# A planner with another model of TensorE's clock, new due dates, and dummy matmuls that share the banks of the attention steps

## The chip, the cores and the metric

The kernel runs on one core of one Trainium2 chip. The time is the device time of one execution in microseconds; the kernel before takes 923.4 us (median of three runs, 922.99 to 923.58).

## What is computed

Attention over q, k, v of shape (4, 8, 576, 64), followed by two MLPs over the 2304 tokens of width 512. The attention is a sum of two parts: one over positions averaged four by four (144 of them, repeated four times at the end), and one in a band of seven positions around each token.

```python
q_d, k_d, v_d = (x.reshape(B, H, S // 4, 4, D).mean(axis=3) for x in (q, k, v))
out_up = np.repeat(sm_attn(q_d, k_d, v_d), 4, axis=2)
mask = np.abs(pos[:, None] - pos[None, :]) < 4
scores = np.where(mask, scale * q @ k.T, -1e9)
out_local = softmax(scores) @ v
x = (out_up + out_local).transpose(0, 2, 1, 3).reshape(2304, 512)
r = np.maximum(x @ w_in, 0.0)               # 512 -> 2048
x = (s * (r * r) + b) @ w_out               # 2048 -> 512
out = ((x @ w_a) * (x @ w_b)) @ w_out2      # 512 -> 1536 -> 512
```

## The kernel before

**The stages.** The *ramp* computes, on TensorE, the averaged attention of batch 0 and batch 1 (`down`, one group for each of four pairs of heads) and the banded attention of the first 768 tokens in six *tile jobs* of 128 tokens (`tile_job`). Tile jobs 0 to 2 fill block 0 of phase A, jobs 3 to 5 block 1. Jobs 0 to 3 lie in batch 0 and read q and k of that batch from buffers that `down` loaded; jobs 4 and 5 load their own (`tq`, `tk`). The band of the other tokens is computed on VectorE (`unit`), beside phase A; each unit visits TensorE for a transpose (`bt`). *Phase A* is the first MLP: six blocks of 384 tokens, each with 16 steps of the hidden width, each step 12 matmuls into `h` (`h_fn`, lines 1154 to 1156) and, two steps later, 12 into `acc` (`o_fn`, lines 1197 to 1199). *Phase B* is the second MLP (line 1443 and lines 1583 to 1585). A value is split into a high and a low fp32r part, and a product is three matmuls: high by high, high by low, low by high.

**The weights.** For block 0 of phase A each of the 32 weight slices (512 KB) comes by SyncE's queue and is split on ScalarE (lines 416, 423 and 452) and VectorE (lines 428, 436 and 457). At most four slices are staged between their transfer and line 436 (the token `stg`). Slices, whole q and k of batch 0 and some other tiles of the ramp share the 33 slots of the pool `w`.

**Steps on TensorE in the ramp.** A down group has scores (`sc`, line 690), transposes (`at`, line 741) and the output (`o`, line 762, evicted at 774 into `up`). A tile job has scores (lines 854 and 862), transposes (line 928) and the output (line 947); VectorE adds `up` (line 964), and the sum is split into `xsh` (ScalarE, line 571) and `xsl` (VectorE, line 575). That is the x that phase A reads.

**The order.** All work stands in a list of tasks (`Program.add`), each with an engine, a planned duration, what it reads, which buffers it takes and gives back, and a due time. `Program.order` plays the list through before the kernel is emitted: it takes again and again the task that can start earliest on its engine, on a tie the one with the smaller due time (less `LEAD` for TensorE's attention steps), and emits in that order. Each engine's queue, SyncE's too, is then run in order by the chip, with semaphores where one engine needs another. Due times are handed back from a task to those that it needs. `target(idx)` is the due time of step idx of phase A: `T0` plus `STEP` per token and step; the jobs' due times hang on it by the constants `DUE_*`.

**PSUM and the dummies.** The eight banks are two `att`, two `h` and four `acc`. An attention step of the ramp takes any of them. `warm_fn` takes one acc bank as `pw` and emits 18 dummy matmuls (bf16, 408 columns) into it; the bank comes free with the first product of phase A. Up to that product `order` also puts dummies ahead of any TensorE step which, by the plan, would otherwise start late: as many as end before the step can start, 20 at most. `Clock` is the plan's model of TensorE's clock: a step runs at full or half speed by what the tick before it did.

Of the kernel before, what the change touches and what calls it, by code (L numbers as in the profile page):

```python
# [7 lines left out]
F32 = mybir.dt.float32  # L8
# [9 lines left out]
HP = H // 2  # L18
# [42 lines left out]
V_ENG = "DDDD"  # L61
POOL_PREP = 2.0
CONST_ENG, DUE_CONST = "G", 8.0
PATIENCE = 0
# [26 lines left out]
class Task:  # L91
    __slots__ = (
        "eng", "dur", "fn", "deps", "succ", "acq", "picks", "rel", "due", "lead", "share", "num", "left", "ready", "start",
        "end", "fill", "seen", "dma", "order", "wait",
# [3 lines left out]
class Clock:  # L98


    TICK, COLUMNS = 3.41333, 1.4

    def __init__(self):
        self.done = {}

    def run(self, start, work, share, keep=True):
        t = start
        while work > 1e-9:
            k = int(t / self.TICK + 1e-6)
            rate = 1.0 if self.done.get(k - 1, 0.0) >= self.COLUMNS else 0.5  # L110
            d = min(work / rate, (k + 1) * self.TICK - t)
            if keep:
                self.done[k] = self.done.get(k, 0.0) + d * rate * share
            work -= d * rate
            t += d
        return t


# [18 lines left out]
class Program:  # L137
# [7 lines left out]

    def add(self, eng, dur, fn, reads=(), writes=(), acq=(), rel=(), due=1e9, after=(), lead=0.0, share=1.0, seen=None, dma=(), order=0, wait=0.0):
# [5 lines left out]
        t.lead, t.share = lead, share  # L152
# [12 lines left out]

    def order(self):
# [8 lines left out]
        at = {e: 0.0 for e in ENGINES}  # L175
        clock, warming, wire = Clock(), True, Wire()
        landed, adding = [], 0.0
        at["SP"] = 0.75
        at["PE"] = clock.run(1.07, 0.17 * WARM, 1.0)
        out = []  # L180
# [107 lines left out]
def moe_chain(ctx, tc, qT, kT, vd, tq, tk, tv, qu, ku, vu, w_a1, w_o1, w_a2, w_b2, w_o2, sb, ident_d, bmask_d, emask_d, out):  # L288
    nc = tc.nc
# [5 lines left out]
    add = P.add  # L295
# [33 lines left out]

# [14 lines left out]
    def warm_fn(picks):  # L344
        V.memset(wz, 0.0)
        pw.append(bank("acc", [128, 408], "pw"))
        keep_warm(WARM)
        V.memset(ones, 1.0)
        A_.activation(out=warm, in_=ones, func=ACTF.Exp)
# [17 lines left out]

    add("CTL", 0.0, warm_fn, acq=[("acc",)], due=-1e6)

# [262 lines left out]
    def down(b, hp, ph, pool_eng, due=1e9):  # L632
# [53 lines left out]
        def s_fn(p):  # L686
# [58 lines left out]

        tt = add("PE", 0.52, t_fn, [("a", key), "ident"], [("at", key)], [wide, wide], lead=LEAD, share=0.5625)

# [9 lines left out]
        def o_fn(p):  # L757
# [9 lines left out]
        to = add(  # L767
            "PE", 2.1 if b == 0 and V_ENG[hp] == "P" else 0.6, o_fn, [("aT", key), ("upslot", b)] + [("dv", key) if b == 0 else ("pv", b)],
            [("o", key)], [wide], [pick(ts, 2)] + ([pick(tv0, 0)] if b == 0 else ["pv"] if hp == HP - 1 else []),
            lead=LEAD, share=0.5625, after=[mm["dO", b, i] for i in range(hp)])  # L770
        mm["dO", b, hp] = to
# [28 lines left out]
    def pick(t, i):  # L800
        return lambda _: t.picks[i]


    def tile_job(i, due):
# [44 lines left out]
        def s_fn(p):  # L849
# [21 lines left out]
            [("tsc", i)], [WIDE, WIDE, ("re",)], () if kept else ["rtq", "rtk"],  # L871
            after=[mm["dS", bl, hp] for hp in range(HP)], lead=LEAD, share=0.55,
        )
# [51 lines left out]
        def t_fn(p):  # L925
# [5 lines left out]
            "PE", 0.55, t_fn, [("ta", i)], [("tat", i)], [WIDE], after=[mm["dT", bl, hp] for hp in range(HP)],  # L931
            lead=LEAD, share=0.75,
        )
# [7 lines left out]
        def o_fn(p):  # L941
# [12 lines left out]
            "PE", 1.45, o_fn, [("taT", i), ("tv", i), ("slot", ("a", blk))] + [("up", b) for b in batches], [("to", i)], [WIDE, WIDE],  # L954
            [pick(ts, 2), pick(t_v, 0)], lead=LEAD, share=0.8,
        )
# [19 lines left out]
    def window(t, R):  # L976
        a = t.rearrange("p r d -> p (r d)")
        return bass.AP(tensor=a.tensor, offset=a.offset, ap=[list(a.ap[0]), [D, R], [D, 7], [1, D]])

    def unit(u, due):  # L980
# [110 lines left out]
        def bt(p):  # L1091
# [4 lines left out]
        tb = add(  # L1096
            "PE", 0.11 * R, bt, [("bo", u), ("slot", ("a", blk))] + [("up", b) for b in batches], [("bt", u)], [ONE],
            ["bo"], lead=LEAD,
        )
# [39 lines left out]
    def a_iter(idx):  # L1139
# [7 lines left out]
        for half in range(2):  # L1147
# [639 lines left out]
```

## Time and profile of the kernel before

| | us |
|---|---|
| median of three runs | 923.4 |
| the profiled execution | 923.98 |
| its span, first to last instruction | 922.2 |
| TensorE (PE) busy | 909.3, 99% |
| VectorE (DVE) busy | 777.4, 84% |
| ScalarE (ACT) busy | 476.2, 52% |
| GpSimd (POOL) busy | 71.8, 8% |
| mean granted TensorE clock | 0.982 of full speed |

In the page, PE is matmul, PEld the weight load beside it, and SPq SyncE's queue, which issues transfers. PEclk is the granted clock as a share of 2.4 GHz; it has two levels, 1.2 and 2.4 GHz, so a stage's value says how much of it ran at which. A matmul that stands in TensorE's queue without a gap counts as busy at either level, so that 99% busy doesn't mean 99% of what the engine could do. The busy time of an engine can hide dummies as well. The table is an average over stages; they are read one by one.

### The profile page before, as it was taken

What the parts mean: (1) busy time and instruction counts of PE and PEld (TensorE: products, weight loads), DVE (VectorE), ACT (ScalarE), POOL (GpSimd) and SP (SyncE); (2) the same over time, 40 slices, a digit from 0 to 9 for tenths busy, and PEclk for the clock granted to TensorE, in tenths of its full rate; (3) what the DMA queues carried; (4) which work ended last, traced back from release to release, by engine and by line L of the source; (5) the groups of instructions that cost most, each with busy time, mean ns of one, the idle gap of its engine ahead of it and who ended that gap; (6) DMA issues with size and microseconds to landing.
All of it is one profiled execution on the core that took longest, in us unless ns stands there. A gap on an engine that the chain in (4) does not pass through costs nothing.

```text
span 922.2 us, 15173 instructions
## 1 busy us (share of the span) xinstructions
PE 909.3 (99%) x5794; PEld 848.4 (92%) x5794; DVE 777.4 (84%) x1390; ACT 476.2 (52%) x1011; POOL 71.8 (8%) x74
## 2 busy tenths in 40 slices
PE   9989999999999999999999999999999999999997
PEld 5779999999999999999998999998999999999996
DVE  8699989999999999996877998779877779877753
ACT  4489974445445445337887454436433335433322
POOL 2310112034222100000000000000000000000000
PEclk9589999999999999999999999999999999999999
DMA  8986744233453323206487132102200000200001
GB/s 250 262 257 204 224 143 137 70 112 119 121 106 118 100 83 106 81 1 231 147 292 265 34 106 69 46 23 84 100 23 24 23 23 12 103 25 23 1 1 69
DMA packets 49224, 97.22 MB, mean 105 GB/s; under 512 B 6592, under 2 KB 24800, under 8 KB 48768
## 3 DMA queue, kind: packets, MB, share of 16 engines
q1 hardware_dynamic: 41520, 93.20, 30.8%
q0 software_dynamic: 7200, 2.67, 2.5%
q8 instruction: 45, 0.74, 0.3%
q10 hardware_dynamic: 432, 0.39, 0.1%
q14 instruction: 27, 0.22, 0.1%
HBM read 83.65 MB, written 12.58 MB: 104 GB/s over the span
## 4 chain that ended last, share of the span: by engine, by line
PE 90%; DVE 6%; ACT 2%; issue 1%; DVEq 0%; ACTq 0%
PE ab L1443 29%; PE h L1154 7%; PE acc L1197 7%; PE h L1155 6%; PE h L1156 6%; PE acc L1198 6%; PE acc L1199 6%; PE acc L1584 5%; PE acc L1585 5%; PE acc L1583 5%; PE pw L328 1%; PE o L762 1%; PE sc L690 1%; PE o L947 1%; PE at L741 1%
## 5 line engine op out<-in xcount | busy, mean ns | idle before, releaser
L1443 PE MATMUL ab<-xo,w 128*128 128x384 f32 x1312 | 267.7, 338 | 1.8 <-DVE w L1507 1.8
L1443 PEld LDWEIGHTS ab<-xo,w 128*128 128x128 f32 x1312 | 235.2, 188 | 16.9 <-DVE w L1507 2.1
L1197 PE MATMUL acc<-gh,w 128*128 128x384 f32 (+1 forms) x384 | 132.1, 344 | 1.5 <-DVE gh L1184 0.9
L1154 PE MATMUL h<-xsh,w 128*128 128x384 f32 x384 | 132.0, 344 | 0.1
L1198 PE MATMUL acc<-gl,w 128*128 128x384 f32 x384 | 129.9, 338 | 0.1
L1155 PE MATMUL h<-xsl,w 128*128 128x384 f32 x384 | 129.9, 338 | 0.0
L1156 PE MATMUL h<-xsh,w 128*128 128x384 f32 x384 | 129.6, 338 | 0.0
L1199 PE MATMUL acc<-gh,w 128*128 128x384 f32 (+1 forms) x384 | 129.5, 337 | 0.0
L1171 ACT ACTIVATE u<-h 128x384 f32<-128x384 f32 x96 | 47.2, 492 | 117.0 <-PE h L1156 113.4
L1559 ACT ACTIVATE gh<-u 128x384 fp32r<-128x384 f32 x68 | 35.7, 524 | 87.3 <-DVE u L1520 50.4
L1197 PEld LDWEIGHTS acc<-gh,w 128*128 128x128 f32 x384 | 72.1, 188 | 3.9 <-ACT w L423 2.0
L1154 PEld LDWEIGHTS h<-xsh,w 128*128 128x128 f32 x384 | 72.8, 190 | 2.2 <-issue 1.8
L1155 PEld LDWEIGHTS h<-xsl,w 128*128 128x128 f32 x384 | 72.9, 190 | 0.0
L1198 PEld LDWEIGHTS acc<-gl,w 128*128 128x128 f32 x384 | 72.2, 188 | 0.7 <-DVE gl L1182 0.7
L1156 PEld LDWEIGHTS h<-xsh,w 128*128 128x128 f32 x384 | 72.8, 190 | 0.0
L1199 PEld LDWEIGHTS acc<-gh,w 128*128 128x128 f32 x384 | 72.2, 188 | 0.0
L1467 ACT ACTIVATE w<-ab 128x384 f32<-128x384 f32 x34 | 16.7, 491 | 100.6 <-PE ab L1443 100.5
L1182 DVE TENSOR_TENSOR gl<-u,gh 128x384 fp32r<-128x384 f32 x96 | 53.6, 558 | 13.7 <-ACT gh L1178 13.3
L1175 ACT ACTIVATE u<-u 128x384 f32<-128x384 f32 x96 | 50.5, 526 | 2.0
L1178 ACT ACTIVATE gh<-u 128x384 fp32r<-128x384 f32 x96 | 50.5, 526 | 1.8
L1443 PE MATMUL ab<-xo,wx 128*128 128x384 f32 x200 | 50.0, 345 | 0.0
L1064 DVE TENSOR_TENSOR pr<-s,bk 128x1792 f32<-128x1792 f32 (+1 forms) x26 | 49.2, 1893 | 0.7
(208 smaller groups left out, 1724.9 us busy)
## 6 DMA issues: line engine op xcount, KB each, us to landing
w<-in_w_o_dram SPq DMA_DIRECT2D x25, 512.0 KB
w<-in_w_a_dram SPq DMA_DIRECT2D x24, 512.0 KB
bk<-in_ku_dram SPq DMA_DIRECT2D x22, 320.0 KB
bk<-in_vu_dram SPq DMA_DIRECT2D x22, 320.0 KB
w<-wod SPq DMA_DIRECT2D x12, 512.0 KB
x2d<-ev SPq DMA_DIRECT2D x24, 192.0 KB
x<-x2d SPq DMA_DIRECT2D x3, 1536.0 KB
w<-in_w_b_dram SPq DMA_DIRECT2D x8, 512.0 KB
```

The costliest lines, as they stand in the source:

```text
L1064: V.tensor_tensor(out=pr, in0=st["s"][:, h].unsqueeze(3).to_broadcast([128, R, 7, D]), in1=window(st["v", h], R), op=ALU.mult,)
L1154: nc.tensor.matmul(out=st["h"], lhsT=w[:, 0, k], rhs=hi[:, k], start=(k == 0), stop=False)
L1155: nc.tensor.matmul(out=st["h"], lhsT=w[:, 0, k], rhs=lo[:, k], start=False, stop=False)
L1156: nc.tensor.matmul(out=st["h"], lhsT=w[:, 1, k], rhs=hi[:, k], start=False, stop=(k == HP - 1))
L1171: A_.activation(out=st["u"], in_=st["h"], func=ACTF.Relu)
L1175: A_.activation(out=st["u"], in_=st["u"], func=ACTF.Square)
L1178: A_.activation(out=st["hi"][:, :n], in_=st["u"], func=ACTF.Copy)
L1182: V.tensor_tensor(out=st["lo"], in0=st["u"], in1=st["hi"][:, :n].bitcast(F32), op=ALU.subtract)
L1197: nc.tensor.matmul(out=acc, lhsT=wh, rhs=st["hi"], start=(f == 0), stop=False)
L1198: nc.tensor.matmul(out=acc[:, :n], lhsT=wh, rhs=st["lo"], start=False, stop=False)
L1199: nc.tensor.matmul(out=acc, lhsT=wl, rhs=st["hi"], start=False, stop=(f == FA - 1))
L1443: nc.tensor.matmul(out=o, lhsT=w[:, k], rhs=x, start=(not more and k + n == 0), stop=(k == 1 and n == 2), skip_group_check=more,)
```

## The change

It touches only what the planner believes, and where the dummies write. (1) New constants: `T0`, `LEAD`, `DUE_*`; `T0` moves every step of phases A and B by 11.7 us. The planned duration of TensorE's steps for batches 2 and 3 and of the units' transposes grows by `VISIT`. (2) `Clock` counts columns of matmuls in place of busy time, with one bound for the first rise and another once it is warm, and `window` sums the columns of the last tick's length before a given time. Each TensorE step carries its columns. (3) `order` puts dummies ahead of a step only if the step asks for them (`fills`; the attention steps of the ramp do, up to 20, phase A's don't), and it goes on adding them after the step could start while the window is short of columns. It counts from when the step's first bank is free. (4) The dummies are emitted by `bank` into the first bank that the step takes, and `pw` is gone: the first 18 take an acc bank that comes free behind them.

```diff
-POOL_PREP = 2.0
-CONST_ENG, DUE_CONST = "G", 8.0
+POOL_PREP, VISIT = 2.0, 0.2
+CONST_ENG, DUE_CONST = "G", 10.9
...
-T0, STEP = 29.1, 4.018 / 384
-LEAD = 28.4
-DUE_DOWN = (12.1, 3.1, 6.3, 19.4)
-DUE_NEXT = (72.9, 0.0)
-DUE_TILE = (9.3, 25, 22.0)
-DUE_JOB = (11.6, 13.1, 12.9)
-
-WARM, FILL_MIN, FILL_MAX = 18, 0, 20
+T0, STEP = 40.8, 4.018 / 384
+LEAD = 21.6
+DUE_DOWN = (15.2, 0.3, 10.5, 19.4)
+DUE_NEXT = (68.9, 0)
+DUE_TILE = (9.3, 24.2, 0.5)
+DUE_JOB = (10.0, 12.7, 6.8)
+
+WARM, FILLS, FILL, FILL_COLUMNS, KEEP_COLUMNS = 18, 20, 0.172, 408, 3179.5
...
-    TICK, COLUMNS = 3.41333, 1.4
...
+    TICK, FIRST, COLUMNS, KEEP, FULL = 3.41333, 3360.0, 2600.0, KEEP_COLUMNS, 2400.0
+
+    def __init__(self, phase=0.0):
+        self.done, self.phase, self.warm, self.past = {}, phase, False, []
+
+    def rate(self, k):
+        if self.done.get(k - 1, 0.0) >= (self.COLUMNS if self.warm else self.FIRST):
+            return 1.0
+        return 0.5
...
+    def window(self, end):
+        total = 0.0
+        for a, b, cols in reversed(self.past):
+            if b <= end - self.TICK:
+                break
+            total += cols * (b - max(a, end - self.TICK)) / (b - a)
+        return total
...
-                g0 = at["PE"]
-                if "acc" in t.rel:
-                    warming = False
-                while warming and t.fill < FILL_MAX and (t.fill < FILL_MIN or clock.run(g0, 0.17, 1.0, False) < s):
-                    g0 = clock.run(g0, 0.17, 1.0)
+                g0 = max(at["PE"], fs[0]) if fs else at["PE"]
+                while t.fill < t.fills:
+                    end = clock.run(g0, FILL, FILL_COLUMNS, False)
+                    if end > s and clock.window(max(s, g0) + t.dur) + t.cols >= clock.KEEP:
+                        break
+                    g0 = clock.run(g0, FILL, FILL_COLUMNS)
                     t.fill += 1
                 t.start = s = max(s, g0)
-                t.end = clock.run(s, t.dur, t.share)
+                t.end = clock.run(s, t.dur, t.cols)
...
+    todo = [0]
+
     def bank(tag, shape, name):
-        return ps.tile(shape, F32, tag=tag, name=name, bufs=4 if tag == "acc" else 2)
-
-    pw = []
-
-    def keep_warm(count):
-
-        for _ in range(count):
-            nc.tensor.matmul(out=pw[0], lhsT=wz[:, :128], rhs=wz, start=True, stop=True)
+        whole = ps.tile([128, 512], F32, tag=tag, name=name, bufs=4 if tag == "acc" else 2)
+
+        for _ in range(todo[0]):
+            nc.tensor.matmul(out=whole[:, :408], lhsT=wz[:, :128], rhs=wz, start=True, stop=True)
+        todo[0] = 0
...
-    add("CTL", 0.0, warm_fn, acq=[("acc",)], due=-1e6)
+    add("CTL", 0.0, warm_fn, acq=[("acc",)], rel=["acc"], due=-1e6)
...
-            "PE", 0.7, s_fn, [("qd", key), ("kd", key)], [("sc", key)], [wide, wide, E_SLOT[ph]],
-            [ph + "qd", ph + "kd"], lead=LEAD, share=0.5)
+            "PE", 0.7 + (VISIT if b > 1 else 0), s_fn, [("qd", key), ("kd", key)], [("sc", key)], [wide, wide, E_SLOT[ph]],
+            [ph + "qd", ph + "kd"], lead=LEAD, cols=648, fills=FILLS if ph == "r" else 0)
...
-            rel = ["acc"] if idx == 0 and half == 0 else []
+            rel = []
...
         for t, picks in P.order():
-            keep_warm(t.fill)
+            todo[0] = t.fill
             t.fn(picks)
```

The other five attention steps get their columns and `fills` in the same way as the one shown.

## Rows read from the trace of the kernel before

**Rows 1.** Stages: length; PE, PEld, DVE, ACT, POOL busy (count); clock, DMA share, GB/s.

```profile
23.40:42.00 18.60, 18.60 (x380) 13.54 (x380) 11.63 (x40) 7.90 (x27) 7.35 (x12) 0.50 1.03 281
42.00:48.00 6.00, 6.00 (x106) 4.39 (x103) 4.58 (x14) 4.29 (x15) 1.19 (x1) 0.96 0.67 152
...
53.50:58.50 5.00, 4.53 (x17) 4.27 (x18) 4.07 (x9) 3.51 (x7) 0.35 (x1) 0.50 1.01 284
...
60.00:104.00 44.00, 42.92 (x433) 40.51 (x432) 42.83 (x93) 43.68 (x91) 4.10 (x3) 1.00 0.80 276
104.00:122.00 18.00, 17.53 (x101) 17.24 (x100) 16.77 (x32) 17.74 (x36) 5.11 (x4) 1.00 0.50 116
...
60.00:65.00 5.00, 4.90 (x89) 4.43 (x88) 4.53 (x12) 4.97 (x11) 1.52 (x1) 1.00 1.03 397
```

**Rows 2.** Chain of waits, 20 to 60 us: start, us, what.

```profile
21.41 0.69 PE at L741 x8
...
26.70 0.34 PE pw L328
27.04 1.17 PE sc L690 x8
28.20 2.37 PE o L947 x64
...
32.26 1.04 PE at L928 x4
...
45.35 0.17 PE pw L328
45.52 0.46 PE at L928 x4
45.98 0.64 PE sc L690 x8
46.63 1.39 PE o L947 x64
48.01 0.64 PE at L741 x8
...
54.91 0.69 PE h L1154
```

**Rows 3.** Timeline of TensorE, 0 to 70 us: start, us, instructions [idle before].

```profile
17.43 0.71 PE L762 MATMUL o<-e,w 72*64 72x144 f32 x8
...
22.04 1.23 PE L762 MATMUL o<-w 72*64 72x144 f32 x8
...
53.91 0.94 PE L741 MATMUL at<-ident,w 72*72 72x72 f32 x6 [1.54 <-issue]
...
67.98 0.41 PE L1197 MATMUL acc<-gh,w 128*128 128x386 f32 x1 [0.93 <-DVE gh L1184]
```

**Rows 4.** Timeline of VectorE, 0 to 130 us.

```profile
53.62 0.74 DVE L964 TENSOR_TENSOR x<-o,up 128x256 f32<-128x256 f32 x2
...
93.31 0.73 DVE L575 TENSOR_TENSOR xsl<-x,xsh 128x512 fp32r<-128x512 f32 x1
```

**Rows 5.** Chain of waits in block 0 of phase A.

```profile
104.64 0.49 ACT u L1171
...
121.25 0.57 ACT w L423
```

**Rows 6.** Dummies alone (line 328), columns as above, PE and PEld only.

```profile
6.00:21.40 15.40, 8.22 (x43) 3.73 (x41) 1.00 0.96 268
21.40:48.00 26.60, 6.26 (x19) 1.95 (x19) 0.62 0.94 242
```

**Rows 7.** Timeline of TensorE, first product of block 1.

```profile
131.50 0.34 PE L1154 MATMUL h<-xsh,w 128*128 128x384 f32 x1
```

**Rows 8.** Waits of SyncE's queue, 0 to 60 us: sum, times, longest.

```profile
SPq L333 <- PE sc L862: 8.2, 1, 8.2
```

**Rows 9.** Timeline of SyncE's queue.

```profile
53.15 0.50 SPq L333 DMA_DIRECT2D w<-in_w_o_dram  x1
```

More of the change, by code (lines that the diff above doesn't have):

```diff
@@ L92 @@
     __slots__ = (
-        "eng", "dur", "fn", "deps", "succ", "acq", "picks", "rel", "due", "lead", "share", "num", "left", "ready", "start",
+        "eng", "dur", "fn", "deps", "succ", "acq", "picks", "rel", "due", "lead", "cols", "fills", "num", "left", "ready", "start",
         "end", "fill", "seen", "dma", "order", "wait",
@@ L98, with run @@
 class Clock:
-    TICK, COLUMNS = 3.41333, 1.4
[L103 to L111, printed above, removed]
+    TICK, FIRST, COLUMNS, KEEP, FULL = 3.41333, 3360.0, 2600.0, KEEP_COLUMNS, 2400.0
[5 more added lines that the diff above has]
+        return 0.5
+    def run(self, start, work, cols, keep=True):
+        t, left, warm = start, work, self.warm
+        while left > 1e-9:
+            k = int((t + self.phase) / self.TICK + 1e-6)
+            rate = self.rate(k)
+            d = min(left / rate, (k + 1) * self.TICK - self.phase - t)
             if keep:
-                self.done[k] = self.done.get(k, 0.0) + d * rate * share
-            work -= d * rate
+                self.done[k] = self.done.get(k, 0.0) + d * rate * cols / work
+                warm = warm or rate == 1.0
+            left -= d * rate
             t += d
-        return t
+        if keep:
+            self.warm = warm
+            self.past.append((start, t, cols))
+            del self.past[:-200]
+        return t
+    def window(self, end):
[5 more added lines that the diff above has]
+        return total
 class Wire:
@@ L144, in __init__, with add @@
         self.free = {k: [0.0] * n for k, n in free.items()}
-    def add(self, eng, dur, fn, reads=(), writes=(), acq=(), rel=(), due=1e9, after=(), lead=0.0, share=1.0, seen=None, dma=(), order=0, wait=0.0):
+    def add(self, eng, dur, fn, reads=(), writes=(), acq=(), rel=(), due=1e9, after=(), lead=0.0, cols=0.0, fills=0, seen=None, dma=(), order=0, wait=0.0):
         t = Task()
@@ L151, in add @@
         t.eng, t.dur, t.fn, t.acq, t.rel, t.due = eng, dur, fn, acq, rel, due
-        t.lead, t.share = lead, share
+        t.lead, t.cols, t.fills = lead, cols or dur * 2190.0, fills
         t.deps, t.order = list(after), list(after) if order else ()
@@ L175, in order @@
         at = {e: 0.0 for e in ENGINES}
-        clock, warming, wire = Clock(), True, Wire()
+        clock, wire = Clock(), Wire()
         landed, adding = [], 0.0
         at["SP"] = 0.75
-        at["PE"] = clock.run(1.07, 0.17 * WARM, 1.0)
+        at["PE"] = clock.run(1.07, FILL * WARM, FILL_COLUMNS * WARM)
         out = []
@@ L318, in new @@
         return pools[ph].tile(shape, dtype, tag=tag, name=tag, bufs=n_bufs[ph][tag])
+    todo = [0]
     def bank(tag, shape, name):
-        return ps.tile(shape, F32, tag=tag, name=name, bufs=4 if tag == "acc" else 2)
-    pw = []
-    def keep_warm(count):
-        for _ in range(count):
-            nc.tensor.matmul(out=pw[0], lhsT=wz[:, :128], rhs=wz, start=True, stop=True)
+        whole = ps.tile([128, 512], F32, tag=tag, name=name, bufs=4 if tag == "acc" else 2)
+        for _ in range(todo[0]):
+            nc.tensor.matmul(out=whole[:, :408], lhsT=wz[:, :128], rhs=wz, start=True, stop=True)
+        todo[0] = 0
+        n = 1
+        for k in shape[1:]:
+            n *= k
+        part = whole[:shape[0], :n]
+        if len(shape) == 3:
+            part = part.rearrange("p (a b) -> p a b", b=shape[2])
+        if len(shape) == 4:
+            part = part.rearrange("p (a b c) -> p a b c", b=shape[2], c=shape[3])
+        return part
     def load(dst_src, nbytes, reads=(), writes=(), acq=(), rel=(), due=1e9, after=(), rows=128, pieces=1, base=0):
@@ L345, in warm_fn @@
         V.memset(wz, 0.0)
-        pw.append(bank("acc", [128, 408], "pw"))
-        keep_warm(WARM)
+        todo[0] = WARM
+        bank("acc", [128, 408], "pw")
         V.memset(ones, 1.0)
@@ L744, in t_fn @@
                         )
-        tt = add("PE", 0.52, t_fn, [("a", key), "ident"], [("at", key)], [wide, wide], lead=LEAD, share=0.5625)
+        tt = add("PE", 0.52 + (VISIT if b > 1 else 0), t_fn, [("a", key), "ident"], [("at", key)], [wide, wide], lead=LEAD, cols=250, fills=FILLS if ph == "r" else 0)
         mm["dT", b, hp] = tt
@@ L767, in down @@
         to = add(
-            "PE", 2.1 if b == 0 and V_ENG[hp] == "P" else 0.6, o_fn, [("aT", key), ("upslot", b)] + [("dv", key) if b == 0 else ("pv", b)],
+            "PE", 2.1 if b == 0 and V_ENG[hp] == "P" else 0.6 + (VISIT if b > 1 else 0), o_fn, [("aT", key), ("upslot", b)] + [("dv", key) if b == 0 else ("pv", b)],
             [("o", key)], [wide], [pick(ts, 2)] + ([pick(tv0, 0)] if b == 0 else ["pv"] if hp == HP - 1 else []),
-            lead=LEAD, share=0.5625, after=[mm["dO", b, i] for i in range(hp)])
+            lead=LEAD, cols=648, fills=FILLS if ph == "r" else 0, after=[mm["dO", b, i] for i in range(hp)])
         mm["dO", b, hp] = to
@@ L871, in tile_job @@
             [("tsc", i)], [WIDE, WIDE, ("re",)], () if kept else ["rtq", "rtk"],
-            after=[mm["dS", bl, hp] for hp in range(HP)], lead=LEAD, share=0.55,
+            after=[mm["dS", bl, hp] for hp in range(HP)], lead=LEAD, cols=684, fills=FILLS if ph == "r" else 0,
         )
@@ L931, in tile_job @@
             "PE", 0.55, t_fn, [("ta", i)], [("tat", i)], [WIDE], after=[mm["dT", bl, hp] for hp in range(HP)],
-            lead=LEAD, share=0.75,
+            lead=LEAD, cols=800, fills=FILLS if ph == "r" else 0,
         )
@@ L954, in tile_job @@
             "PE", 1.45, o_fn, [("taT", i), ("tv", i), ("slot", ("a", blk))] + [("up", b) for b in batches], [("to", i)], [WIDE, WIDE],
-            [pick(ts, 2), pick(t_v, 0)], lead=LEAD, share=0.8,
+            [pick(ts, 2), pick(t_v, 0)], lead=LEAD, cols=608, fills=FILLS if ph == "r" else 0,
         )
@@ L1096, in unit @@
         tb = add(
-            "PE", 0.11 * R, bt, [("bo", u), ("slot", ("a", blk))] + [("up", b) for b in batches], [("bt", u)], [ONE],
-            ["bo"], lead=LEAD,
+            "PE", 0.11 * R + VISIT, bt, [("bo", u), ("slot", ("a", blk))] + [("up", b) for b in batches], [("bt", u)], [ONE],
+            ["bo"], lead=LEAD, cols=800,
         )
```

## The prediction

> **What bounds the kernel now.** I read the table by stages first [rows 1]. From 60 us to the end TensorE is busy almost without a break (42.92 of 44 us in 60 to 104, and the later stages look alike), so no later stage has much to give: what can move is the ramp before the first product of phase A, and how ScalarE and VectorE keep up behind it. The stage 23.4 to 42 us is the odd one: TensorE is busy for all 18.60 us, at a granted clock of 0.50, that is at the lower of its two levels, 1.2 GHz. VectorE works only 11.63 us of it and ScalarE 7.90. Next I read the chain of waits [rows 2]. From 21.41 to 48.65 us it lies on TensorE alone, in 32 pieces: 23 of attention steps and 9 of dummies. The same step stands there at both levels: scores of a down group 1.17 and 0.64 us, the output of a tile job 2.37 and 1.39, its transposes 1.04 and 0.46. The nine dummy pieces (first 0.34, last 0.17) sum to 5.19 us; as they lie in the chain they covered no wait on the chip, whatever the plan thought.
>
> Behind the chain of TensorE comes a short wait: eight transposes of a down group begin late, at 53.91, after 1.54 us in which TensorE stood still [rows 3]. The releaser is given as "issue", but an addition of a tile job on VectorE (line 964), which frees the banks of that job's output, begins 0.29 us before [rows 4]. I read it as a wait for a PSUM bank; seven of the eight banks circulate in the ramp, since pw keeps one of the acc banks until the first product. The first product of phase A begins at 54.91 [rows 2], and the clock is at the lower level there too: 0.50 in 53.5 to 58.5 [rows 1].
>
> Last, who is late next. In 60 to 104 ScalarE is busy 43.68 of 44 us and VectorE 42.83; in 104 to 122 ScalarE is busy 17.74 of 18 [rows 1], and from 104.64 to 121.25 the chain runs through ScalarE's splitting of the weights and VectorE's share of it, not through TensorE [rows 5]. So ScalarE, VectorE and TensorE are all three close to the bound in block 0 of phase A. A ramp shortened for TensorE alone would only make TensorE wait there.
>
> **The change, part by part.**
> *The plan's clock.* Nothing of it is emitted; it moves the times at which the planner believes that a step ends, so the order in the in-order queues, and the count of dummies. Worth of the clock in the ramp, from the chain and TensorE's own list [rows 2, 3]: two tile outputs at 2.37 where 1.39 is possible, 2.0 us; three score steps at 1.17 for 0.64, 1.6; two transposes at 1.04 for 0.46, 1.2; two outputs of a down group at 1.23 for 0.71, 1.0. Together 5.8 us; the score steps of tiles, which change little, are left out. At the start of phase A, 54.9 to 58.5 at half speed loses 1.8 us.
>
> *The dummies.* They are now allowed before every attention step of the ramp, even where they put the step off, so as to keep the clock. 43 dummies stood in 6 to 21.4 us, where the clock held, at 8.22 us busy, 0.19 each; only 19 in 21.4 to 48, where it fell [rows 6]. What they cost on the chain is not shown by the trace of before. From below: all lie in waits, and the 5.2 us of now go as well. From above: the density of the first stretch (2.8 per us) over the 24.6 us from 23.4 to 48 is 69, 50 more than now, and half of them on the chain at 0.19 are 4.8 us. I take the middle: they cost on the chain what they cost now, a change of zero.
>
> *The bank.* The dummies go into the bank of the step behind them, and pw's bank comes free after the first 18. Eighth bank: 1.5 us of the wait above. In exchange a dummy waits for the last reader of its bank, which pw's never did; the step, and all that is queued behind it on TensorE, waits for that bank anyway, so the cost is not the wait but the uncovered gap, in which the clock may fall. Bound: nothing, or the fall of rival two.
>
> *The due dates.* Relative to phase A (which moves by 11.7 us), tile jobs 3, 4 and 5 fall due 21 to 23 us later, batch 1's down groups 4.0 us later. Work that is only moved behind the first product gains nothing by itself on TensorE. Its cover: the last x of job 5 is split at 93.31 and block 1 first reads its x at 131.50 [rows 4, 7], 37 us later; job 5's shift of 21.5 leaves some 16. Without that cover block 1 would wait, us for us. Their transfers move too. SyncE's queue held for 8.2 us behind the score step of a tile job [rows 8], which holds the slot of the next job's queries, and the weight load behind it went out only at 53.15 [rows 9]. Jobs due later should come behind more weights, so that ScalarE and VectorE find weights in the ramp. That is what can save their time; the size follows.
>
> *LEAD, VISIT, DUE_CONST, DUE_JOB.* They turn ties and place TensorE's visits behind 122 us. TensorE's largest wait in phase A is 0.93 us [rows 3]; I bound this at one such wait either way and take zero.
>
> **The sum.** In 23.4 to 48 us TensorE could save 5.8. What is late next there: VectorE, with 7.0 + 1.4 = 8.4 us idle in the two stages, would allow 8.4; the DMA engines are full in 23.4 to 42 (share 1.03 at 281 GB/s, so 5.2 MB), and at the 397 GB/s that they reach in 60 to 65 us they would need 13.2 us for the same bytes, which allows 5.4 [rows 1]. So 5.4 there. Bank 1.5; start of phase A, half of 1.8, 0.9, since the first products follow a wait for operands and their own steps get no dummies. Together 7.8 us earlier in TensorE's own account. ScalarE has to find those 7.8 us in its idle time of the ramp, 10.7 + 1.7 = 12.4 us in the same two stages [rows 1], with weights that have landed; its gaps are broken into pieces by waits for VectorE and TensorE. I take 60 in 100: 4.7 us. Profiled execution 923.98 us (span 922.2): 919.3. The median of the runs shown is 0.6 us below the profiled one: 918.7 us. Ends: all that VectorE allows plus the bank is 9.9 us, 913.5; on the other side the rivals.
>
> **Rivals.**
> *One: the dummies eat what the clock gives.* The clock holds, but the plan's slack is not the chip's and 25 more dummies stand in the chain, 4.8 us against 5.8. For it: the nine pieces that stand in the chain now. Against it: those were placed by a plan that took the steps at another speed. Only 1.0 us is left at most: 922.5 us, no change. Chance 0.18.
>
> *Two, slower: the clock falls all the same and the dummies run slow.* Place: 23 to 48 us. A dummy stands behind its bank's eviction, so the gap before it is uncovered; the clock falls as it does now, and the 25 extra dummies on the chain cost not 0.19 but 0.34 (one piece in the chain [rows 2]): 8.5 us, less the bank's 1.5, less what ScalarE and VectorE make of the longer ramp by splitting weights, for which I take half of the rest: +3.5, 927 us. It decides where banks come free later than operands. For it: the waiting pieces of now include one for a bank, and the clock fell in spite of a planner that had a clock. Against: one more bank, and a falling clock is just what the new count of dummies looks at. The Trainium skill speaks for this rival: "TensorE: Matmul & The Clock Gate", Part 1, says that the chip's observation of activity runs freely and does not start with the kernel, and warns against fitting counts to it. A plan that starts its ticks with the kernel would then meet the chip's by luck, and the time would be that of this rival. The three runs of before, 922.99 to 923.58, show no such scatter, so the trace bears it out little. Chance 0.17.
>
> *Three: block 1 or its x is late.* ScalarE and VectorE, full in block 0, push the moved jobs past their 16 us of remaining slack. It would cost the excess, some 3 us: 926 us. Chance 0.05.
>
> **How the numbers follow.** Forecast 0.60 with its own range of 913 to 921. A change within 0.2%, 1.8 us, is about what a measurement of this kernel can tell from none. Faster 0.61 (the forecast and the better edge of rival one), same 0.18, slower 0.21. The range of 8 in 10 reaches from 913.0, the end above, to 926.0: it takes in rivals one and three and the mild cases of two.
>
> **What would show it.** Right: a granted clock near 1.00 in 23 to 48 us and at the first products; scores at 0.64 and tile outputs at 1.39 there; the first product of phase A before 49 us; the wait for a bank before it gone; ScalarE still full up to about 118 us, block 0 ending 4 to 5 us sooner and the gain unchanged from there to the end. Wrong: 0.50 again in that stretch with more dummies in the chain (rival two); a high clock but the first product still behind 53 us (one); or TensorE waiting for ScalarE or VectorE by several us between 60 and 130, which would mean that the ramp's gain was given back.

## Result, and the profile after

| | before | after |
|---|---|---|
| median of the runs, us | 923.4 (922.1 to 923.6, 5 runs) | 928.4 (927.8 to 932.9, 5 runs) |
| ratio after to before, 95% interval | | 1.0065 [1.0042, 1.0089] |
| profiled execution, us (its span) | 923.98 (922.2) | 927.76 (925.6) |
| granted clock, mean of the profiled span | 0.982 | 0.995 |

The changed kernel is 0.65% slower by the ratio of the runs (5 us between the medians). The forecast was 918.7 us, and its range ended at 926.0: both are missed, and the sign with them. Yet the clock rose as forecast up to 42 us. So the first question is where the time went after the ramp had been mended.

The stages of after, with the columns of [rows 1] (length; TensorE, its weight loads, VectorE, ScalarE, GpSimd busy with their counts; granted clock, DMA share, GB/s):

```profile
23.40:42.00 18.60, 15.04 (x407) 10.56 (x407) 16.25 (x52) 12.84 (x43) 10.62 (x14) 1.00 1.03 277
42.00:48.00 6.00, 6.00 (x52) 4.02 (x48) 3.44 (x7) 3.13 (x7) 3.14 (x3) 0.72 1.01 217
...
53.50:58.50 5.00, 4.58 (x31) 4.23 (x30) 5.00 (x16) 5.00 (x15) 0.97 (x1) 1.00 0.96 253
60.00:104.00 44.00, 43.50 (x437) 41.25 (x436) 42.46 (x90) 43.56 (x90) 6.97 (x5) 1.00 0.81 271
104.00:122.00 18.00, 18.00 (x161) 17.63 (x160) 17.42 (x35) 17.61 (x37) 3.59 (x3) 1.00 0.49 91
```

From 23.4 to 42 us the clock is at its upper level all through, where before it was at the lower one [rows 1]; VectorE does 16.25 us of work there instead of 11.63 and ScalarE 12.84 instead of 7.90. In 60 to 104 us ScalarE is full, as before. Dummies alone, TensorE's columns as in [rows 6]; they are at line 345 now:

```profile
6.00:21.40 15.40, 8.31 (x44) 3.84 (x43) 1.00 0.97 260
21.40:48.00 26.60, 9.06 (x36) 3.26 (x34) 0.94 1.01 256
```

There are 36 of them behind 21.4 us, not 19. TensorE's list (start, length, line, operation, count, idle time before it and its releaser), to be laid beside [rows 2, 3, 7]:

```profile
28.77 1.46 PE L974 MATMUL o<-e,tv 38*64 38x32 f32 x64
...
32.65 0.71 PE L717 MATMUL sc<-kd,qd 64*72 64x144 f32 x8
...
38.48 0.66 PE L889 MATMUL sc<-w 64*32 64x38 f32 x51
41.88 0.29 PE L889 MATMUL sc<-w 64*32 64x38 f32 x13 [2.74 <-issue]
...
51.85 0.44 PE L1181 MATMUL h<-xsh,w 128*128 128x384 f32 x1
...
75.78 0.96 PE L789 MATMUL o<-w,pv 72*64 72x144 f32 x12 [0.50 <-DMA pv<-in_vd_dram]
...
128.57 0.34 PE L1181 MATMUL h<-xsh,w 128*128 128x384 f32 x1
```

A tile output takes 1.46 us (2.37 before), a score step 0.71 (1.17); the first product of phase A starts at 51.85 instead of 54.91, 3.1 us sooner. One long gap is left in the ramp, 2.74 us ahead of 41.88, and the clock falls once behind it (0.72 in 42 to 48). The row at 75.78 is new: TensorE waits for pv, the pooled v of batch 1, which it did not wait for before. The wait is 0.50 us, and no fall of the clock follows it (1.00 in 60 to 104).

To see where the lead of 3 us goes I followed a mark through phase A: the start of ScalarE's first operation on the result h of the n-th step. Difference to before's profiled execution, in us (negative is sooner). The kernels named e are the experiments of the next section.

| n (before at, us) | 0 (59.2) | 8 (100.4) | 20 (151.6) | 40 (247.9) | 60 (343.1) | 95 (491.7) |
|---|---|---|---|---|---|---|
| after | -4.3 | -3.7 | -2.3 | -6.4 | -0.4 | +3.4 |
| e1, without VISIT | -4.0 | +3.0 | +4.4 | -0.8 | +1.5 | +3.8 |
| e8, VISIT alone | -0.2 | -0.1 | -0.3 | +7.8 | +9.2 | +8.9 |
| e9, due dates alone | -6.0 | +4.2 | +5.6 | +1.5 | +3.2 | +7.3 |
| e7, pv planned later | -8.1 | -4.3 | -3.3 | -5.2 | -2.7 | -0.5 |
| e6, both | -6.3 | -6.4 | -5.4 | -10.7 | -8.5 | -6.5 |

Two places stand out. Kernels that run into a long wait for pv, 2.3 us or more, lose 7 to 10 us between n = 0 and 8 (e1, e9). Kernels with VISIT at 0.2 lose 2.8 to 9.1 us between n = 20 and 95 (after 5.7, e7 2.8, e8 9.1), where those without stay within -1.1 and +1.7. (The dip at n = 40 is work that the new due dates put behind it: it is made up by n = 95, and e3, with the old dates, goes from +2.8 to +2.6 there.)

Each line of the table is one execution. Those of e1 (928.15 us), e5 (929.30) and e9 (931.23) are among the slowest of their kernels' runs, those of after (927.76), e6 (916.89) and e12 (922.16) the fastest, so differences between lines are larger than those between medians. The n = 0 column is scatter in part. The kernels' planner, played through, gives after, e1, e5, e6, e7 and e13 the same instructions in the same order on every engine up to 68 us of planned time, and yet their first products start at 51.85, 52.12, 52.77, 49.77, 47.94 and 49.73 us. The gap ahead of 41.88 shows where they part: each of these kernels stops inside that score step, after the 51st of its 64 matmuls, for 2.74, 3.02, 4.39, 0.32, 1.37 and 0.64 us. Of e1 and e6:

```profile
37.15 0.65 PE L889 MATMUL sc<-w 64*32 64x38 f32 x51
40.83 0.37 PE L889 MATMUL sc<-w 64*32 64x38 f32 x13 [3.02 <-issue]
```

```profile
40.33 0.81 PE L891 MATMUL sc<-w 64*32 64x38 f32 x51
41.45 0.29 PE L891 MATMUL sc<-w 64*32 64x38 f32 x13 [0.32 <-issue]
```

A stop in the middle of this step, at the same instruction each time, is no wait for a PSUM bank: both banks of the step had been written before, by the mask matmuls of line 881. Nor is the wait of [rows 3] that the prediction read as one: of the eight transposes two had already run, into the same bank as the next two.

```profile
52.05 0.32 PE L741 MATMUL at<-ident,w 72*72 72x72 f32 x2
```

One queue of the page goes with these stops, the one that the profile calls "instruction" (packets, MB, share):

```profile
q8 instruction: 45, 0.74, 0.3%
```

By the packets' times in the traces, one of its 16 KB packets ends 1.3 to 1.7 us before TensorE goes on in each of the 18 such stops of 0.4 us or more between 20 and 60 us in all the traces (at 40.24 for 41.88 in after, at 52.52 for 53.91 in before). I read the stops as TensorE out of instructions; no run changed this alone.

### The profile page after: what moved, and what is told of

Same layout as the page of the kernel before. It is cut to its first block, busy times and chain, and to the rows that moved or that the text cites. A ratio compares the mean times of both kernels' runs of the same rounds, so it can differ in the third digit from the quotient of the medians.

```text
span 925.6 us, 15217 instructions
## 1 busy us (share of the span) xinstructions
PE 906.2 (98%) x5812; PEld 842.1 (91%) x5812; DVE 776.7 (84%) x1390; ACT 476.8 (52%) x1011; POOL 74.7 (8%) x74
## 4 chain that ended last, share of the span: by engine, by line
PE 72%; DVE 15%; issue 7%; DMA 2%; ACT 1%; POOL 1%; SPq 0%; DVEq 0%; POOLq 0%; ACTq 0%
PE ab L1470 29%; PE acc L1611 5%; PE acc L1612 5%; PE acc L1610 5%; PE acc L1224 4%; PE acc L1225 4%; PE h L1181 4%; PE acc L1226 4%; PE h L1182 4%; PE h L1183 4%; DVE pr L1030 2%; DVE s L1036 2%; DVE gl L1209 2%; DVE pr L1091 2%; DVE pr L1098 1%
## 5 line engine op out<-in xcount | busy, mean ns | idle before, releaser
L1470 PEld LDWEIGHTS ab<-xo,w 128*128 128x128 f32 x1330 | 239.1, 189 | 18.1 <-DVE w L1534 2.4
L1494 ACT ACTIVATE w<-ab 128x384 f32<-128x384 f32 x30 | 14.7, 491 | 99.0 <-PE ab L1470 96.9
L455 DVE TENSOR_SCALAR w<-w 128x512 uint16<-128x512 f32 x60 | 44.6, 760 | 7.9 <-ACT w L450 7.9
L1030 DVE TENSOR_TENSOR pr<-bq,bk 128x1792 f32<-128x1792 f32 (+1 forms) x26 | 49.2, 1891 | 1.2 <-DMA bq<-in_qu_dram 0.8
```

The lines of the kernel that those rows point to most:

```text
L1030: V.tensor_tensor(out=pr, in0=st["q", h].unsqueeze(2).to_broadcast([128, R, 7, D]), in1=window(st["k", h], R), op=ALU.mult,)
L1470: nc.tensor.matmul(out=o, lhsT=w[:, k], rhs=x, start=(not more and k + n == 0), stop=(k == 1 and n == 2), skip_group_check=more,)
```

## Experiments

The theories. *Order*: the ramp is better, but VISIT, a length of 0.2 us added to the planner's TensorE steps, makes a looser order behind 122 us. *Supply*: the new plan asks for pv before its DMAs can have landed. *Rival*: the ramp itself costs the time, its dummies, its banks or its new clock. Each run is compared with before on the same chip. There were three chips: the median of before was 923.6 us beside e1 to e5, 924.5 beside e6 to e9 and 922.9 beside e10 to e13, 23 to 29 runs each. Kernels measured on different chips are compared by their ratios to before, and so is after, whose chip is not on record.

### e1: VISIT back to zero; e3: the ramp's clock and dummies with the old dates

```diff
# e1, against after
-POOL_PREP, VISIT = 2.0, 0.2
+POOL_PREP, VISIT = 2.0, 0.0
# e3, against e1
-T0, STEP = 40.8, 4.018 / 384
+T0, STEP = 29.1, 4.018 / 384
-LEAD = 21.6
+LEAD = 28.4
-DUE_DOWN = (15.2, 0.3, 10.5, 19.4)
+DUE_DOWN = (12.1, 3.1, 6.3, 19.4)
...
```

In e3 DUE_NEXT, DUE_TILE, DUE_JOB and DUE_CONST are those of before as well.

> The changed kernel with VISIT at zero; ramp as in the changed kernel, only the order of the visits for batches 2 and 3 and the units moves. Theory one (order: what is lost between 280 and 500 us comes from where the new plan puts these visits): 923 to 925 us, with TensorE's idle time in 280 to 360 us below the 2.1 us of the changed kernel. Theory two (supply: phase A starts earlier but VectorE can't deliver sooner, so any order gives the ramp's gain back behind it): about 928 us, unchanged.

Measured: 924.6 us (10 runs, 921.9 to 929.1), ratio 1.0009 [0.9986, 1.0032]. VISIT costs after 0.56%, some 5 us, but without it the kernel is no faster than before. That is the theory of the order, and TensorE's idle time in 280 to 360 us falls from 2.1 us to 0.1, as it said. The runs spread over 7 us. The profiled one, with a span of 926.3 us, is one of the longer ones. Its wait for pv in TensorE's list, then the busy times with the columns of the table by stages:

```profile
77.85 1.71 PE L789 MATMUL o<-w,pv 72*64 72x144 f32 x12 [2.30 <-DMA pv<-in_vd_dram]
```

```profile
60.00:104.00 44.00, 41.70 (x401) 38.77 (x400) 36.70 (x78) 37.51 (x76) 6.05 (x4) 0.88 0.73 241
78.00:90.00 12.00, 12.00 (x59) 10.67 (x60) 6.77 (x13) 7.50 (x16) 1.41 (x1) 0.58 0.37 117
```

TensorE waited 2.30 us, and behind the wait the clock is at the lower level: 0.58 on average in 78 to 90 us, though TensorE is busy for all 12 us of it. A mean of 0.88 over 44 us is about 10 us at half speed, so 5 us lost. The mark of the table has the same: from -3.3 us at n = 4 to +3.0 at n = 8. ScalarE and VectorE, which had been full there, fall to 37 of 44 us.

> The change without its constants: the new clock model and the dummies in the steps' banks, with the old T0, LEAD and due dates and VISIT at zero. Theory one (order): the clock holds in the ramp, first product of phase A near 52 us, and the old due dates lose little behind it: 919 to 922 us. Theory two (supply): first product near 52 us, and by 430 us phase A is where it was before: 923 to 924 us.

Measured: 930.4 us (7 runs), 1.0058 [1.003, 1.0087], slower than either theory had it. First product at 51.81, as in after; then the same trouble as in e1, and more of it:

```profile
72.82 3.63 PE L789 MATMUL o<-w,pv 72*64 72x144 f32 x28 [3.62 <-DMA pv<-in_vd_dram]
```

So the wait for pv does not need the new due dates. The planner puts batch 1's output at 67.1 us here, ahead of the 69.5 in before, and TensorE stands there from 69.2 us on.

### e4, e9: the new due dates with the old clock model and dummies; e5: part of the old dates in after

```diff
# e4, against before
-POOL_PREP = 2.0
+POOL_PREP, VISIT = 2.0, 0.2
...
-T0, STEP = 29.1, 4.018 / 384
+T0, STEP = 40.8, 4.018 / 384
...
# e9, against e4
-POOL_PREP, VISIT = 2.0, 0.2
+POOL_PREP, VISIT = 2.0, 0.0
# e5, against after
-POOL_PREP, VISIT = 2.0, 0.2
+POOL_PREP, VISIT = 2.0, 0.0
-LEAD = 21.6
+LEAD = 28.4
-DUE_DOWN = (15.2, 0.3, 10.5, 19.4)
+DUE_DOWN = (15.2, 0.3, 6.3, 19.4)
-DUE_JOB = (10.0, 12.7, 6.8)
+DUE_JOB = (11.6, 13.1, 12.9)
```

e4 has all the constants of the change, LEAD and every due date among them, and VISIT on the same steps.

> The kernel before with the new constants only: T0, LEAD, the due dates, DUE_CONST and VISIT; old clock model and the dummies in pw's bank. Theory one (order): the clock falls in the ramp as before, and behind it some 5 us are lost: 927 to 931 us. Theory two (supply): with a ramp as long as before there is nothing to give back: 923 to 925 us.

> The new due dates, T0 and LEAD without VISIT, with the old clock model and pw. Theory of pv and VISIT: about 4 us below e4's 928.7, so 923.5 to 925.5 us. Rival, the due dates themselves cost what e4 lost: 927.5 to 929 us.

> The changed kernel with only the part that serves the ramp: VISIT zero, and LEAD, DUE_JOB and the third and fourth of DUE_DOWN (which hold behind the ramp) as before. Theory one (order): the ramp's 3 us stay: 919 to 921 us, first product at about 52 us. Theory two (supply): 923 us or more, the gain of 3 to 4 us at 100 us used up by 430 us.

Measured: e4 928.7 us (10 runs), 1.0055 [1.0041, 1.007]; e9 926.3 (12 runs), 1.0027 [1.0012, 1.0043]; e5 926.5 (10 runs), 1.0033 [1.0014, 1.0053]. e4 and e5 lie where the theories of the order and of the supply had them; e9 lies between its two. e9 has its first product at 47.63 us, sooner than after, with the planner's old clock: the dates alone, which take work out of the ramp, shorten it. It loses the lead at the same place, TensorE's list again:

```profile
79.10 2.67 PE L762 MATMUL o<-w,pv 72*64 72x144 f32 x20 [4.11 <-DMA pv<-in_vd_dram]
```

and has about 10 us at the lower clock behind it, and so has e5 behind the same wait. Neither half of the change is free of it, so none of these runs speaks for the rival yet, and e4 against e9 prices VISIT once more, at 0.28%, 2.6 us. In e4 itself the wait for pv is 0.67 us.

### e6, e7: tell the plan that pv lands later, without VISIT and with it

The planner is told that the last accumulation of batch 1's pv is usable 8 us after the time it works out. Nothing else is touched, and the DMAs are the same.

```diff
# e6, against after; e7 is the same with VISIT = 0.2
-POOL_PREP, VISIT = 2.0, 0.2
+POOL_PREP, VISIT = 2.0, 0.0
...
-                u.ready = max(u.ready, s + ISSUE if t in u.order else t.end + (0.0 if u.eng == t.eng == "PE" else t.seen))
+                u.ready = max(u.ready, s + ISSUE if t in u.order else t.end + t.late + (0.0 if u.eng == t.eng == "PE" else t.seen))
...
+                if b == 1 and r == 3:
+                    t[kh].late = 8.0
```

> VISIT zero as in e1, and the plan is told that the pooled v of batch 1 (pv) is of use 8 us later than it computes, so TensorE's queue holds other work where it waited in e1. Theory of pv and VISIT: no wait of TensorE for the DMA of pv, no fall of the clock between 60 and 104 us, 919.5 to 921.5 us, runs closer together than e1's 921.9 to 929.1. Rival, supply (VectorE gives the ramp's gain back): 923.5 us or more.

> The changed kernel (VISIT 0.2) with the same 8 us for pv. Theory of pv and VISIT: the slow ones of its runs go (930 to 933), what VISIT costs stays: 925 to 926.5 us. Rival, that pv's wait is rare and small: 928 us as the changed kernel.

Measured: e6 919.1 us (6 runs, 916.9 to 921.2), 0.9943 [0.9924, 0.9961]; e7 923.1 (12 runs), 0.998 [0.9964, 0.9997]. e6 is faster than both kernels, and the only one of the twelve whose whole interval lies more than 0.2% below before (e7 and e13, at 0.20 and 0.27%, reach nearly up to it). e7 is faster than either expectation. Planning pv later is worth 0.66% (e1 to e6) or 0.85% (after to e7), 6.1 or 7.8 us, by kernels on different chips; VISIT costs 0.37% (e6 to e7) or 0.56% (e1 to after), 3.4 or 5.2 us. The two together are the way from 0.9943 to 1.0065, 11.3 us. e6's list, and its stage 60 to 104 us with the columns as above:

```profile
49.77 0.44 PE L1183 MATMUL h<-xsh,w 128*128 128x384 f32 x1
...
80.64 1.70 PE L791 MATMUL o<-w,pv 72*64 72x144 f32 x24
```

```profile
60.00:104.00 44.00, 43.81 (x485) 41.52 (x478) 42.75 (x91) 43.84 (x91) 6.67 (x4) 1.00 0.76 248
```

No wait for pv, the clock stays up in this stage, and the lead of 6.3 us at n = 0 is still 6.5 at n = 95. e7's profiled run still waits 1.39 us for pv, longer than after's, and the clock falls (0.72 in 78 to 90): its first product came at 47.94, so TensorE is there sooner. What e7 has ahead of after at n = 0, 3.9 us, is as much as it has at n = 95 (3.9) and lies in the part that the two kernels share. So these two traces don't show that the later pv is what makes e7 faster; e1's and e6's do, with 2.3 us of their difference in the shared part too.

Why pv is late can be read in GpSimd's list. The pooled v is summed by six DMAs that accumulate one after the other on GpSimd's queue, and each goes out when the one before has landed: the time in brackets is most of that wait (only the one at 45.17 has other work of GpSimd ahead of it). Of before, the third to the sixth:

```profile
43.28 1.19 POOL L625 DMA_DIRECT2D pv<-in_vd_dram  x1 [6.99 <-issue]
48.19 1.20 POOL L625 DMA_DIRECT2D pv<-in_vd_dram  x1 [3.72 <-issue]
52.65 1.19 POOL L625 DMA_DIRECT2D pv<-in_vd_dram  x1 [3.27 <-issue]
63.39 1.52 POOL L625 DMA_DIRECT2D pv<-in_vd_dram  x1 [9.55 <-issue]
```

and of after:

```profile
45.17 1.21 POOL L652 DMA_DIRECT2D pv<-in_vd_dram  x1 [1.16 <-issue]
53.27 1.20 POOL L652 DMA_DIRECT2D pv<-in_vd_dram  x1 [6.90 <-issue]
61.30 1.19 POOL L652 DMA_DIRECT2D pv<-in_vd_dram  x1 [6.83 <-issue]
71.31 1.69 POOL L652 DMA_DIRECT2D pv<-in_vd_dram  x1 [8.82 <-issue]
```

In before two of the waits are 3.72 and 3.27 us: they lie where its DMA engines were less busy (share 0.67 in 42 to 48 us [rows 1], 0.25 at 32 GB/s in 48 to 53.5). In after the engines are nearly full from 23 to 58 us (0.89 to 1.03): SyncE's queue, held for 8.2 us in before [rows 8], is held for 3.2 there, and no wait behind 45.17 is under 6.8. The last one goes out at 71.31 instead of 63.39. But it lands within 4.1 us of that, where before's took 10.9: by the packets' times it has landed at 75.44 in after and at 74.25 in before, 1.2 us apart (at 77.48 in e1, 78.12 in e9). The larger part is that TensorE starts the step at 74.82 instead of 79.17:

```profile
79.17 2.34 PE L762 MATMUL o<-w,pv 72*64 72x144 f32 x32
```

That row is before's: there the step had been supplied for 4.9 us. The kernel's own planner puts this step at 69.5 us in before and at 68.8 in after, so hardly apart; but in before phase A ran 8 us behind the plan (46.8 planned, 54.91 on the chip), and this error covered the other one. In e6 pv lands at 80.52, just ahead of the 80.64 of its step. That the full DMA engines slow the accumulations is read from these rows; no run changed the load alone.

### e8: VISIT alone in the kernel before

```diff
# against before
-POOL_PREP = 2.0
+POOL_PREP, VISIT = 2.0, 0.2
...
-            "PE", 0.11 * R, bt, [("bo", u), ("slot", ("a", blk))] + [("up", b) for b in batches], [("bt", u)], [ONE],
+            "PE", 0.11 * R + VISIT, bt, [("bo", u), ("slot", ("a", blk))] + [("up", b) for b in batches], [("bt", u)], [ONE],
```

The three TensorE steps of the down groups with b > 1 get it too, as in the change.

> The kernel before with VISIT at 0.2 and nothing else. Theory of pv and VISIT: 927 to 929 us, with waits of TensorE for VectorE between 200 and 500 us that the kernel before doesn't have. Rival, VISIT costs only where phase A starts earlier (supply): 923 to 924.5 us.

Measured: 933.3 us (6 runs), 1.0104 [1.0081, 1.0128], so 9 us slower for a number that emits no instruction, and more than was expected. Busy times of 200 to 280 us, first before, then e8 (columns as above), and e8's list there:

```profile
200.00:280.00 80.00, 79.36 (x498) 75.13 (x498) 77.02 (x102) 36.85 (x95) 21.85 (x18) 1.00 0.43 111
```

```profile
200.00:280.00 80.00, 74.59 (x444) 69.93 (x443) 78.41 (x108) 36.11 (x90) 20.89 (x17) 0.96 0.44 115
```

```profile
204.51 0.66 PE L1094 MATMUL bt<-ident,o 128*128 128x128 f32 x4 [0.78 <-ACT e L717]
205.64 0.45 PE L1197 MATMUL acc<-gh,w 128*128 128x384 f32 x1 [0.47 <-ACT gh L1178]
208.75 0.69 PE L1198 MATMUL acc<-gl,w 128*128 128x384 f32 x1 [2.67 <-DVE gl L1182]
```

The steps themselves are no longer; TensorE waits, here for VectorE and ScalarE, and the clock is at 0.96. I read it as an order that leaves them work at times when the plan holds TensorE for busy. VISIT stands on 37 steps between steps 20 and 95 of phase A, 7.4 us, and by the kernel's own planner this stretch grows from 336 us to 344 (after, e4, e7) or 350 (e8). The chip follows it: 340 us before, 339 in e6, 343 to 346 in after, e4 and e7, 349 in e8. By the planner these 37 steps still interrupt phase A 34 to 37 times, so TensorE is not spared what VISIT was to price. In after TensorE's waits from 120 to 500 us are 4.4 us, in before 1.2, in e1 0.5. The largest of after in 230 to 330 us, from the view of waits (sum, times, longest):

```profile
PE at L768 <- DVE e L759: 1.1, 1, 1.1
PE at L768 <- ACT u L1198: 0.5, 1, 0.5
PE bt L1121 <- DVE o L1106: 0.5, 1, 0.5
PE at L768 <- DVE m L1064: 0.4, 1, 0.4
```

### e10, e11, e12: what the parts of the ramp are worth, each taken out of e6

```diff
# e10, against e6: dummies only where the plan sees TensorE idle
-WARM, FILLS, FILL, FILL_COLUMNS, KEEP_COLUMNS = 18, 20, 0.172, 408, 3179.5
+WARM, FILLS, FILL, FILL_COLUMNS, KEEP_COLUMNS = 18, 20, 0.172, 408, 0.0
# e11, against e6: dummies in a bank of their own, held to the first product
-    add("CTL", 0.0, warm_fn, acq=[("acc",)], rel=["acc"], due=-1e6)
+    add("CTL", 0.0, warm_fn, acq=[("acc",)], due=-1e6)
-            rel = []
+            rel = ["acc"] if idx == 0 and half == 0 else []
-                g0 = max(at["PE"], fs[0]) if fs else at["PE"]
+                g0 = at["PE"]
...
```

In e11 the dummies go out just ahead of the step, into that one bank. e12 is e9 (old clock model, dummies and bank, the new dates, VISIT 0) with pv planned 8 us later, as in e6.

> e6 with the bound for the window at zero: dummies only where the plan sees TensorE idle, never to hold the clock. If holding the clock is what shortens the ramp: the clock falls between 21 and 48 us for 10 us or more, first product of phase A at 53 us or later, 922 to 925 us. If the new order does it: 919 to 920 us as e6.

> e6 with the dummies in a bank of their own (pw, held until the first product of phase A) as in the kernel before; clock model and due dates of the change. If the eighth bank is worth what the prediction gave it (1.5 us): 920 to 921.5 us, with waits of TensorE for banks before 52 us. If it is worth nothing: 918.5 to 919.5 us.

> The new due dates without VISIT on the old clock model and pw (e9), with the 8 us for pv. If the clock model, the dummies and the bank carry e6's gain: 922.5 to 924.5 us, the clock falling in the ramp as in the kernel before. If the due dates carry it: 919 to 920.5 us. Below e9's 926.3 in both, since TensorE no longer waits for pv.

Measured: e10 928.2 us (6 runs), 1.0063 [1.0042, 1.0084]; e11 924.5 (12 runs), 1.002 [1.0005, 1.0035]; e12 925.6 (12 runs), 1.0022 [1.0004, 1.004]. Each is slower than was expected of it, and slower than e6. By the ratios to before, holding the clock is worth 1.20% in this plan, 11.1 us, the steps' own banks and the eighth bank 0.77%, 7.1, clock model with dummies and banks 0.79%, 7.3. Against e13 below, which ran on their chip and differs from e6 by one number, it is 0.90, 0.47 and 0.49%. Either way the rival falls: the ramp's parts pay. The stages of e10, columns as above:

```profile
23.40:42.00 18.60, 16.84 (x328) 13.32 (x325) 15.31 (x44) 13.50 (x42) 10.79 (x13) 0.53 1.01 274
...
48.00:60.00 12.00, 10.32 (x155) 8.63 (x154) 11.23 (x25) 9.61 (x24) 1.20 (x1) 0.50 1.03 268
```

The clock is at the lower level nearly all the time from 23.4 to 60 us, longer than in before (which had 0.96 in 42 to 48 us [rows 1]), and the first product comes at 55.46. In e11 the waits of TensorE from 21 to 60 us (sum, times, longest) have

```profile
PE sc L897 <- issue: 3.2, 1, 3.2
PE h L1189 <- ACT w L752: 1.5, 1, 1.5
```

and the first product comes at 53.81. The 3.2 us are a stop inside the score step, after 48 of its 64 matmuls, like that of after and e1: no wait for a bank. e12 begins phase A at 48.50, before e6, but its clock is at 0.91 in 42 to 48 and 0.75 in 53.5 to 60 us: an early start at the wrong clock, and the lead is down to 2.0 us at n = 95. It has no wait for pv, where e9 waited 4.11 us in its slowest run, and yet the two kernels are alike in their ratios, 1.0022 and 1.0027: with the old clock model planning pv later gained nothing that can be told from none.

### e13: 12 us instead of 8

```diff
# against e6
-                    t[kh].late = 8.0
+                    t[kh].late = 12.0
```

> e6 with 12 us for pv in place of 8. If what is left of e6's and e7's scatter comes from pv: 918 to 919 us, no run above 921, no wait of TensorE for the DMA of pv. If not: as e6, 919.1 us, with the same spread.

Measured: 920.9 us (12 runs, 916.5 to 924.1), 0.9973 [0.9948, 0.9998]. No wait for pv, and yet a spread of 7.5 us, with runs above 921: the expectation that pv makes the scatter failed. The profiled run (921.5 us) waits elsewhere, with a fall of the clock behind it (0.89 in 130 to 145 us):

```profile
135.42 0.69 PE L1226 MATMUL acc<-gh,w 128*128 128x384 f32 x1 [2.20 <-ACT ev L1253]
```

So what scatters between runs of one kernel is not pv alone. A wait of about 2 us in this kernel may or may not drop the clock: behind one of 2.14 us ahead of 38.22 in e3 it stayed at 1.00.

## Why the prediction was wrong, point by point

- **What bounds the kernel: right.** The ramp was the place, and behind it ScalarE is full (43.56 of 44 us).
- **The plan's clock, the dummies: the mechanism right, the size open.** Granted clock 1.00 from 23.4 to 42 us, steps at the shorter durations, 17 more dummies; e10, with fewer, is slower. But the clock fell in 42 to 48 us (0.72), and the first product came at 51.85, not before 49. How much shorter the ramp is can't be read from one execution: the same instructions gave first products from 47.94 (e7) to 52.77 (e5). That e6 comes out at 0.9943 of before, where the sum had 918.7 of 923.4, 0.9949, is partly luck: the sum holds 1.5 us for a wait that it misread, and e13, the same up to 68 us of the plan, came out at 0.9973. What the prediction had not seen is that the new dates alone shorten the ramp too (first product 47.63 in e9): the parts do not add up, and without the clock the dates gain nothing (e12).
- **The bank: the reading failed.** The 1.5 us were taken from a wait that is no wait for a bank but a stop inside a step, and after has such a stop of 2.74 us though no bank is set aside for the dummies. No run shows a wait for the eighth bank. Taking the new banks out of e6 costs more than 1.5 us all the same, 0.77% (0.47 against e13); the planner has the first product 1.9 us later there (48.5 for 46.6), and the rest stays open.
- **The due dates: one of two steps that failed.** The prediction named batch 1's down groups and looked only at transfers of x and weights. GpSimd's six accumulating DMAs that feed them were never priced, nor was it asked when TensorE would reach them once the ramp was shorter. It took earlier weights as a pure gain; they fill the stretch in which pv used to land sooner. In e1, e3, e5 and e9 the wait is 2.30 to 4.11 us with a fall of the clock behind it, in e6 it is gone at 0.66% less than e1. For after itself the size is open: its trace has 0.50 us and no fall of the clock, its slower runs (930.51 and 932.88 us) left none, and planning pv later brought from 0.05% (e9 to e12) to 0.85% (after to e7). What the prediction did fear there, block 1 without its x (rival three), did not happen: the last x is split at 119.99 and first read at 128.57, without a wait, but the cover shrank from 37 us [rows 4, 7] to 8.6, where 16 had been worked out.
- **"LEAD, VISIT, DUE_CONST, DUE_JOB ... take zero": the other step that failed, and the one shown most plainly.** The bound was taken from the largest wait on the chip, as if the constants could only move a step by that. VISIT lengthens the plan by 7.2 us, and every engine's queue is filled by the plan. By single edits it costs 0.56% in after, 0.37% in e7 and 1.04% in before (5.2, 3.4 and 9.6 us); in after's trace the lead shrinks by 5.7 us between n = 20 and 95. For LEAD and DUE_JOB no effect is shown (e5 1.0033 and e1 1.0009, with intervals that overlap).
- **"The gain unchanged from there to the end": wrong** for after (-2.3 us at n = 20, +3.4 at n = 95), right for e6 (-5.4, -6.5).
- **Rivals.** The first (dummies eat the gain) is contradicted by e10. The second had the right sign and nearly the time, 927 us, mostly for another reason: in after the clock did fall in its place, but only in 42 to 48 us (0.72), which at half speed for 3.4 us loses 1.7, and behind a stop, not behind a bank. Against it the prediction held the narrow scatter of three runs. That was too strong: beside the experiments before itself ran from 919.9 to 930.4 us, and within a kernel the runs with a higher mean clock were on the whole the shorter ones (e1: clock 0.995 to 0.997 in the three of 921.9 to 922.6 us, 0.988 to 0.990 in the three of 928 to 929, but also 0.990 in one of 923.2). The Trainium skill's page "TensorE: Matmul & The Clock Gate", Part 1, says that the observation runs freely and does not start anew with a kernel. No run here separates that from the other causes of the scatter, such as the stops of varying length in the ramp.
- **The sum** misses by 1.16%, 10.7 us. VISIT accounts for 3.4 to 5.2 of it. The rest, 0.60% by e1, is what e6 makes good; how it divides between the wait for pv and the scatter of the ramp is not shown.

## What to carry to other kernels

When a ramp is shortened, follow every operand of the first steps behind it back to its queue, the accumulating transfers first, and ask how long they take under the new load and when they will now be asked for: an error of the plan may be what covers them today. A number that only the planner sees is not free; price it by how many steps carry it, since the chip runs at the pace of the order that comes out. And hold a small constant apart from a large change when it is tried: between after, 0.65% slower than before, and e6, 0.57% faster, stand one constant and one planned landing. Do not read the length of a ramp from one execution: here the same instructions scattered over 4.8 us before phase A began.

## What the runs showed that had not been expected

- A 144 KB accumulating DMA on GpSimd's queue let the next one go 3.3 to 3.7 us later in before while the DMA engines were less busy, and 6.8 to 9.6 us later in before and after while they were nearly full. (One in e3 took 3.9 us at a share of 1.05, so the share alone does not settle it.)
- A wait of 2.3 us cost 5 us more in clock: about 10 us at the lower level, with TensorE busy for the whole of the 12 us from 78 to 90. In other runs waits of like length cost less (2.74 us at 41.88 in after: 0.72 in 42 to 48; 2.20 at 135.42 in e13: 0.89 in 130 to 145) or nothing (2.14 at 38.22 in e3).
- TensorE stopped inside a step, at the same instruction in every kernel with the same order, for 0.32 to 4.39 us, each time until 1.3 to 1.7 us after a packet of the instruction queue had ended.
